# The first step of a fused GELU block by halves of its rows, and its operands in single transposing loads

## Chip, cores and metric

The kernel runs on one core of a Trainium2 chip. The metric is device time in microseconds (us), the median of three runs. The profile is one further execution, taken by the hardware profiler; its span is the time from the first to the last instruction that it records. PE is the matrix engine, DVE the vector engine, ACT the scalar engine, POOL the GpSimd engine, and SP the engine that issues most of the DMA loads.

## What is computed

The reference is the forward pass of a two-layer block with tanh-GELU and all its gradients. The core of it:

```python
h   = einsum("bsd,df->bsf", x, w1) + b1      # B=1, S=2048, D=448, F=1792, all bf16
h   = gelu(h, approximate=True)
out = einsum("bsf,fd->bsd", h, w2) + b2
_out, _vjp = jax.vjp(_f, x, w1, b1, w2, b2)
grads = _vjp(grad_out)                       # for x, w1, b1, w2, b2
```

So there are six matrix products: u = x w1 and out = h w2 forward, the product of grad_out with w2 transposed, the gradient of x from the gated result, and the gradients of w1 and w2 as sums over all rows. The gradients of b1 and b2 are sums over rows.

## The kernel before

**Tiling.** The 2048 rows are four blocks of 512 (SB). F is 14 tiles of 128; a step handles two of them, so a block has 7 steps (NPAIR) and the main loop 28 (g). D is 448, which is three tiles of 128 and a rest of 64 (DL). x, grad_out (g), w1 and w2 transposed (w2T) stand in SBUF with D on the partitions: tiles 0 to 2 are full, tile 3 (KF) is the rest. For x and w1 the three full tiles are columns 64 to 447 and the rest is columns 0 to 63, in partitions 0 to 63; for g and w2T the full tiles are columns 0 to 383, and the rest is in partitions 64 to 127. The two rests therefore use different halves of the array's rows and run beside each other.

**Loads.** `load_x`, `load_g` and `load_w2T` (lines 137 to 156) each issue two transposing DMAs from SP's queue: one of the three full tiles and one of a single tile of 128 columns that covers the rest. SP's queue is in order and carries, one after the other, x and g of block 0, w2T, w2 and w1 piece by piece (lines 170 to 205), then x and g of block 1 and w1 transposed. The first piece of w1 (columns 0 to 255) comes over ACT's queue behind b1, the second over POOL's queue behind a memset. Loads of blocks 2 and 3 are issued in the main loop, in the third step of the block before (line 412). Each load waits until the block that last used its buffer is done with it.

**b1.** It is loaded as one row into one partition (line 171); 14 matmuls of one row against a one (line 184) turn it into a column per tile, which DVE copies to `b1_col` (line 185). Zero matmuls around these ("warm", lines 180 and 187) keep PE busy until the data arrive.

**A step.** `M1(g)` (line 218) is the three full tiles of u for two tiles of F, `rest` (line 229) the two rests of u for the next step and of q for this one, `M4(g)` (line 242) the full tiles of q, the product of g with w2T. ACT copies u with the bias into V (`act_first`, line 248), squares it into A and takes the GELU into the ring hT. DVE forms Bt from A and V (line 269), ACT its tanh (line 272), DVE the slope factor p from A and hT (line 276) and, by lines 277 to 279, t. The gate (`dve_gate`, line 282) multiplies t with q into ghT. V, A, Bt, u and q have one buffer each; t and p have two. The main loop (from line 373) issues for step g: the rests, M4(g), the gate, then the copies, squares and GELU of step g+1, DVE's and ACT's later parts for g+1, the pieces of the output products (`run_pieces`, line 337), and M1(g+2). Every engine works its own queue in the order of issue.

**The first step.** Lines 367 to 372 run ahead of the loop: M1(0) and its rest into two PSUM tiles; `first_step` (line 256), which copies one half of u by ACT and the other by DVE and squares each by itself; tanh, slope and product at full width; then M1(1). In step 0 four keep-warm matmuls (line 384) stand between the rests and M4(0).

**After the loop.** POOL loads x and g again with rows on partitions (lines 422 and 423), SP turns hT back from DRAM (line 435), and PE forms the gradients of w1 (lines 471 and 479) and w2 (line 490). POOL also issues the stores of hT during the loop (`store_h`, line 284) and of the outputs (`evict`, line 321).

Of the kernel before, what the change touches and what calls it, by code (L numbers as in the profile page):

```python
# [8 lines left out]
ACT = mybir.ActivationFunctionType  # L9
# [9 lines left out]
def kernel(  # L19
# [79 lines left out]
    def xq(b):  # L99
        o = (b % 2) * 2 * KD * SB  # L100
        return xg_flat[:, o:o + KD * SB].rearrange("p (k s) -> p k s", k=KD)
# [32 lines left out]

    def load_x(b):
        rows = slice(b * SB, (b + 1) * SB)
        nc.sync.dma_start_transpose(out=xq(b)[:, 0:KF, :], in_=x2[rows, DL:D])
        nc.sync.dma_start_transpose(out=xq(b)[:, KF, :], in_=x2[rows, 0:P])  # L140

    def load_g(b):
        rows = slice(b * SB, (b + 1) * SB)
        nc.sync.dma_start_transpose(out=gq(b)[:, KF, :], in_=g2[rows, DOV:D])
        nc.sync.dma_start_transpose(out=gq(b)[:, 0:KF, :], in_=g2[rows, 0:DM])

    def load_w1(eng, f0, f1):
        eng.dma_start(out=w1_sb[:, 0:KF, f0:f1], in_=w1[DL:D, f0:f1].rearrange("(k p) f -> p k f", p=P))
        eng.dma_start(out=w1_sb[0:DL, KF, f0:f1], in_=w1[0:DL, f0:f1])

    def load_w2(eng, t0, t1):
        eng.dma_start(out=w2_sb[:, t0:t1, :], in_=w2[t0 * P:t1 * P, :].rearrange("(t p) d -> p t d", p=P))

    def load_w2T(f0, f1):
        nc.sync.dma_start_transpose(out=w2T_sb[:, KF, f0:f1], in_=w2[f0:f1, DOV:D])
        nc.sync.dma_start_transpose(out=w2T_sb[:, 0:KF, f0:f1], in_=w2[f0:f1, 0:DM])

    def load_w1T(t0, t1):
        nc.sync.dma_start_transpose(out=w1T_sb[:, t0:t1, :], in_=w1[:, t0 * P:t1 * P])

    warm = T_flat[:, 0:SB]
    ones = T_flat[0:1, SB:SB + 1]
    b1_row = T_flat[0:1, 4 * SB:4 * SB + F]
    nc.vector.memset(warm, 0.0)
    nc.vector.memset(ones, 1.0)
    nc.vector.memset(w128[:], 1.0 / P)

    nc.gpsimd.memset(gh_nat[:, NB - 1, 0:6, :], 0.0)
    load_w1(nc.gpsimd, 256, 512)
    load_x(0)  # L170
    nc.scalar.dma_start(out=b1_row, in_=b1.rearrange("(o f) -> o f", o=1))
    load_w1(nc.scalar, 0, 256)
    nc.scalar.activation(out=T_flat[0:1, SB + 2:SB + 3], in_=ones, func=ACT.Gelu_apprx_tanh)
    load_g(0)
    load_w2T(0, 256)
    load_w2(nc.sync, 0, 2)
    load_w1(nc.sync, 512, 768)
    pw = psum_a.tile([P, SB], F32, name="acc")
    for i in range(7):
        nc.tensor.matmul(pw[:], lhsT=warm[:, 0:P], rhs=warm, start=True, stop=True)  # L180

    pb = psum_a.tile([P, SB], F32, name="acc")
    for ft in range(NF):
        nc.tensor.matmul(pb[:, ft:ft + 1], lhsT=b1_row[:, ft * P:(ft + 1) * P], rhs=ones, start=True, stop=True)
    nc.vector.tensor_copy(out=b1_col[:], in_=pb[:, 0:NF])
    for i in range(3):
        nc.tensor.matmul(pw[:], lhsT=warm[:, 0:P], rhs=warm, start=True, stop=True)
    load_w2T(256, 512)
    load_w2(nc.sync, 2, 4)
    load_w1(nc.sync, 768, 1280)  # L190
    load_w2T(512, 768)
    load_w2(nc.sync, 4, 8)
    load_w2T(768, 1024)
    load_w1(nc.sync, 1280, F)
    load_w2T(1024, 1280)
    load_w2(nc.sync, 8, NF)
    load_w2T(1280, 1536)
    load_x(1)
    load_w2T(1536, F)
# [18 lines left out]
    def M1(g):  # L218
        if g == 0:
            u_of[g] = [psum_a.tile([P, SB], F32, name="acc")[:] for h in range(2)]  # L220
        else:
            u = psum_u.tile([P, 2, SB], F32, name="u")
            u_of[g] = [u[:, h, :] for h in range(2)]
        for h in range(2):
            for kt in range(KF):
                nc.tensor.matmul(u_of[g][h], lhsT=w1_sb[:, kt, cols(g, h)], rhs=xq(g // NPAIR)[:, kt, :],  # L226
                                 start=(kt == 0), stop=False, skip_group_check=True)

    def rest(gu, gg):

        if gg is not None:
            q = psum_g.tile([P, 2, SB], F32, name="q")
            g_of[gg] = q
        for h in range(2):
            if gu is not None:
                nc.tensor.matmul(u_of[gu][h], lhsT=w1_sb[0:DL, KF, cols(gu, h)], rhs=xq(gu // NPAIR)[0:DL, KF, :],  # L236
                                 start=False, stop=True, tile_position=(0, 0), skip_group_check=True)
            if gg is not None:
                nc.tensor.matmul(q[:, h, :], lhsT=w2T_sb[DL:P, KF, cols(gg, h)], rhs=gq(gg // NPAIR)[DL:P, KF, :],
                                 start=True, stop=False, tile_position=(DL, 0), skip_group_check=True)  # L240

    def M4(g):
        for h in range(2):
            for kt in range(KF):
                nc.tensor.matmul(g_of[g][:, h, :], lhsT=w2T_sb[:, kt, cols(g, h)], rhs=gq(g // NPAIR)[:, kt, :],  # L245
                                 start=False, stop=(kt == KF - 1), skip_group_check=True)

    def act_first(g):
        u = u_of.pop(g)
# [3 lines left out]
        nc.scalar.activation(out=A_of(g), in_=V_of(g), func=ACT.Square, scale=math.sqrt(3.0 * GELU_C * GELU_A))  # L253
        nc.scalar.activation(out=hT(g), in_=V_of(g), func=ACT.Gelu_apprx_tanh)  # L254

    def first_step(g):

        u = u_of.pop(g)
        nc.scalar.activation(out=V_of(g)[:, 0, :], in_=u[0], func=ACT.Identity, bias=b1_col[:, 0:1])
        nc.vector.tensor_scalar(out=V_of(g)[:, 1, :], in0=u[1], scalar1=b1_col[:, 1:2], scalar2=None, op0=ALU.add)  # L260
        for h in range(2):
            nc.scalar.activation(out=A_of(g)[:, h, :], in_=V_of(g)[:, h, :], func=ACT.Square,
                                 scale=math.sqrt(3.0 * GELU_C * GELU_A))
            nc.vector.scalar_tensor_tensor(out=B_of(g)[:, h, :], in0=A_of(g)[:, h, :], scalar=3.0 * GELU_C,
                                           in1=V_of(g)[:, h, :], op0=ALU.add, op1=ALU.mult)
        nc.scalar.activation(out=hT(g), in_=V_of(g), func=ACT.Gelu_apprx_tanh)  # L266

    def dve_first(g):
        nc.vector.scalar_tensor_tensor(out=B_of(g), in0=A_of(g), scalar=3.0 * GELU_C, in1=V_of(g), op0=ALU.add, op1=ALU.mult)  # L269
# [9 lines left out]
        nc.vector.tensor_tensor(out=t_of(g), in0=t_of(g), in1=p_of(g), op=ALU.mult)  # L279

    def dve_gate(g):
        nc.vector.scalar_tensor_tensor(out=ghT(g), in0=t_of(g), scalar=1.0, in1=g_of.pop(g)[:], op0=ALU.add, op1=ALU.mult)  # L282

    def store_h(g):
        b, c = blk(g)
# [35 lines left out]
    def evict(un):  # L321
        key = (un.kind, un.b, un.j // 2)
        if key not in stage:
            stage[key] = iop.tile([P, 2, D], BF16, name="io_" + un.kind)
        st = stage[key]
        if un.by_act:
            nc.scalar.copy(out=st[:, un.j % 2, :], in_=un.ps[:, 0:D])
        else:
            nc.vector.tensor_tensor(out=st[:, un.j % 2, :], in0=un.ps[:, 0:D], in1=b2_bc[:], op=ALU.add)  # L329
        dst = out2 if un.kind == "o" else gx2  # L330
        if un.j % 2:
            r0 = un.b * SB + (un.j - 1) * P
            nc.gpsimd.dma_start(out=dst[r0:r0 + 2 * P, :].rearrange("(j p) d -> p j d", p=P), in_=st[:])  # L333

    full = []
# [28 lines left out]
            turns.setdefault(at, []).append((b, c0, c1))  # L364
    stored = 0

    M1(0)
    rest(0, None)
    first_step(0)
    act_second(0)  # L370
    dve_second(0)
    M1(1)
    for g in range(NSTEP):
        b, c = blk(g)
        pieces = [U[k] for k in seq[b] for _ in range(NF)]
        n = len(pieces)
        own = pieces[n * c // NPAIR:n * (c + 1) // NPAIR]
        grown = [U[k] for k in grow[b] for _ in range(2)]
        nxt = g + 1 if g + 1 < NSTEP else None
        rest(nxt, g)  # L380
        if g == 0:

            for i in range(4):
                nc.tensor.matmul(pw[:], lhsT=w1_sb[:, 0, 0:P], rhs=xq(0)[:, 0, :], start=True, stop=True)
        M4(g)
        flush(False)
        dve_gate(g)
        if nxt is not None:
            act_first(nxt)
        flush(True)  # L390
        if nxt is not None:
            dve_first(nxt)
        last = b == 0 and c == NPAIR - 1
        if last:
            run_pieces(grown + own)
            flush(True)
        if nxt is not None:
            act_second(nxt)
            dve_second(nxt)
        if g == NPAIR:  # L400
            run_pieces(grown)
            M1(g + 2)
            run_pieces(own)
        elif not last:
            run_pieces(grown + own)
        if g != NPAIR and g + 2 < NSTEP:
            M1(g + 2)
        for _ in range(2):
            if g >= NPAIR - 1 and stored < g:
                store_h(stored)  # L410
                stored += 1
        if c == 2 and 0 < b < NB - 1:
            load_x(b + 1)
            load_g(b + 1)
        for t in turns.get(g, []):
            turn_gh(*t)
# [2 lines left out]
    flush()  # L419


    nc.gpsimd.dma_start(out=x_all, in_=x2.rearrange("(st p) d -> p st d", p=P))
    nc.gpsimd.dma_start(out=g_all, in_=g2.rearrange("(st p) d -> p st d", p=P))
    for k in "og":
        for j in range(SPB):
            un = U[k, NB - 1, j]
# [103 lines left out]
```

## Time and profile before

| What | Value |
|---|---|
| Median of three runs | 275.95 us (275.45 to 275.96) |
| Profiled execution | 275.59 us |
| Its span | 273.8 us, so 1.79 us lie around it |
| Busy share of the span: PE, DVE, ACT, POOL | 98%, 69%, 52%, 20% |
| Chain that ended last, by engine | PE 82%, DVE 12%, ACT 2%, DMA 2%, issue 1% |
| Transposing loads by SP: x, g, w2T | 8, 8 and 14 issues |
| Data moved | 43.78 MB at a mean of 160 GB/s |

A line of a timeline gives the start and length in us, the engine, the line of the kernel, the operation, what it writes and reads, its shape and how many are merged; in brackets stands how long the engine had been idle before it, and what released it. "SPq" is SP's queue, and the length is then the time that the issue took, not that of the transfer. The chain of waits gives start, length, engine, tile and line of the work that ended last, followed back from the end. Where an engine is busy on this chain, shortening its work there moves the end, until another engine takes its place.

### The profile page before, as it was taken

How to read it: one execution, taken by the hardware profiler on the slowest of the kernel's cores; microseconds unless marked ns; L12 is line 12 of the kernel's file. 1: busy time of each engine (PE TensorE's matmuls, PEld its weight loads, DVE VectorE, ACT ScalarE, POOL GpSimd, SP SyncE). 2: the span in 40 equal slices, each digit the busy share in tenths (PEclk: the TensorE clock that was granted, in tenths of full speed). 3: DMA queues.
4: the chain of work that ended last, by engine and by line, in shares of the span. 5: the costliest groups of instructions: out<-in, count | busy, mean ns of one | idle time of the engine just before them, and what ended most of it. 6: DMA issues, size and time to landing. Idle time of an engine off the chain costs nothing.

```text
span 273.8 us, 3596 instructions
## 1 busy us (share of the span) xinstructions
PE 267.6 (98%) x1406; PEld 123.7 (45%) x1406; DVE 189.3 (69%) x218; ACT 143.7 (52%) x188; POOL 54.6 (20%) x57
## 2 busy tenths in 40 slices
PE   7899999999999999999999999999999999999995
PEld 3343434443444344444444445554445655555552
DVE  0799999999999999999888871139999970000000
ACT  2878879788888778887777740011111221112111
POOL 6000002730301403033031135111700019400000
PEclk9999999999999999999999999999999999999999
DMA  7878979999999928055534339999999931101111
GB/s 164 172 190 193 213 117 170 274 317 246 199 242 203 249 58 163 24 154 122 138 113 79 110 105 217 325 335 241 165 201 273 225 100 57 44 9 50 50 51 35
DMA packets 101379, 43.78 MB, mean 160 GB/s; under 512 B 90353, under 2 KB 97905, under 8 KB 101362
## 3 DMA queue, kind: packets, MB, share of 16 engines
q1 hardware_dynamic: 94272, 26.68, 51.6%
q0 software_dynamic: 4544, 14.92, 16.9%
q10 hardware_dynamic: 2546, 1.95, 2.5%
q8 instruction: 11, 0.18, 0.3%
q14 instruction: 6, 0.05, 0.1%
HBM read 7.00 MB, written 14.23 MB: 78 GB/s over the span
## 4 chain that ended last, share of the span: by engine, by line
PE 82%; DVE 12%; ACT 2%; DMA 2%; issue 1%; DVEq 0%
PE acc L313 27%; PE acc L490 16%; PE acc L471 13%; PE q L245 10%; PE u L226 9%; PE u L236 4%; DVE Bt L269 3%; DVE T L276 3%; DVE ghT_h L282 3%; PE acc L479 2%; DMA xg_h<-in_x_dram 2%; DVE T L279 2%; DVE T L277 1%; DVE T L278 1%; ACT VA L252 1%
## 5 line engine op out<-in xcount | busy, mean ns | idle before, releaser
L313 PE MATMUL acc<-w_gw,hT_h 128*128 128x448 bf16 x224 | 46.3, 352 | 0.2 <-ACT VA L252 0.2
L313 PE MATMUL acc<-w1T_gw,ghT_h 128*128 128x448 bf16 x224 | 45.1, 352 | 0.0
L245 PE MATMUL q<-xg_h,w2T_g 128*128 128x512 bf16 x168 | 41.1, 381 | 0.0
L252 ACT ACTIVATE VA<-u,b_col 128x512 f32<-128x512 f32 x54 | 34.0, 679 | 13.5 <-PE u L236 12.9
L226 PE MATMUL u<-xg_h,w_x 128*128 128x512 bf16 x162 | 39.4, 379 | 0.8 <-DMA w_x<-in_w_dram 0.4
L282 DVE SCALAR_TENSOR_TENSOR ghT_h<-T,q 128x1024 bf16<-128x1024 bf16 x28 | 34.2, 1221 | 8.4 <-PE q L245 7.0
L272 ACT ACTIVATE T<-Bt 128x1024 bf16<-128x1024 f32 x28 | 29.6, 1056 | 13.9 <-DVE Bt L269 13.8
L471 PE MATMUL acc<-gh_nat,w_x 128*128 128x512 bf16 (+1 forms) x192 | 36.7, 353 | 0.0
L276 DVE SCALAR_TENSOR_TENSOR T<-VA,hT_h 128x1024 bf16<-128x1024 f32 x28 | 34.1, 1219 | 0.2 <-ACT hT_h L266 0.2
L269 DVE SCALAR_TENSOR_TENSOR Bt<-VA 128x1024 f32<-128x1024 f32 x27 | 32.9, 1219 | 0.0
L313 PEld LDWEIGHTS <-hT_h 128*128 128x128 bf16 x224 | 21.9, 98 | 22.0 <-issue 0.5
L313 PEld LDWEIGHTS <-ghT_h 128*128 128x128 bf16 x224 | 21.9, 98 | 20.9
L456 DVE TENSOR_TENSOR VA<-VA,gh_nat 128x1792 f32<-128x1792 f32 x14 | 30.0, 2142 | 0.5
L253 ACT ACTIVATE VA<-VA 128x1024 f32<-128x1024 f32 x27 | 28.5, 1057 | 0.9
L254 ACT ACTIVATE hT_h<-VA 128x1024 bf16<-128x1024 f32 x27 | 28.1, 1040 | 0.0
L471 PEld LDWEIGHTS <-w_x 128*128 128x128 bf16 x192 | 18.7, 98 | 17.8 <-issue 0.4
L245 PEld LDWEIGHTS <-w2T_g 128*128 128x128 bf16 x168 | 14.2, 97 | 24.9 <-issue 11.4
L226 PEld LDWEIGHTS <-w_x 128*128 128x128 bf16 x168 | 16.3, 98 | 20.0 <-DMA w_x<-in_w_dram 1.4
L492 ACT CAST w_gw<-acc 128x448 bf16<-128x448 f32 x13 | 6.9, 532 | 32.6 <-PE acc L490 32.6
L333 POOL DMA_DIRECT2D out_dram<-io_o x8 | 5.8, 727 | 90.3 <-DVE io_o L329 48.6
L473 ACT CAST w1T_gw<-acc 128x512 bf16<-128x512 f32 (+1 forms) x12 | 6.3, 532 | 30.1 <-PE acc L471 24.2
L286 POOL DMA_DIRECT2D hT_dram<-hT_h x28 | 20.3, 728 | 1.9 <-DMA out_dram<-io_o 1.9
(60 smaller groups left out, 234.6 us busy)
## 6 DMA issues: line engine op xcount, KB each, us to landing
hT_dram<-hT_h POOLq DMA_DIRECT2D x28, 256.0 KB, 4.5
out_dram<-io_o POOLq DMA_DIRECT2D x8, 224.0 KB, 5.0
out_dram<-io_g POOLq DMA_DIRECT2D x8, 224.0 KB, 3.6
w_x<-in_x_dram POOLq DMA_DIRECT2D x1, 1792.0 KB, 10.8
w2T_g<-in_grad_out_dram POOLq DMA_DIRECT2D x1, 1792.0 KB, 14.7
out_dram<-w_gw SPq DMA_DIRECT2D x4, 336.0 KB, 2.4
w_x<-in_w_dram SPq DMA_DIRECT2D x2, 384.0 KB, 4.0
out_dram<-w1T_gw ACTq DMA_DIRECT2D x2, 384.0 KB, 5.4
```

What stands on the lines that cost most here:

```text
L226: nc.tensor.matmul(u_of[g][h], lhsT=w1_sb[:, kt, cols(g, h)], rhs=xq(g // NPAIR)[:, kt, :], start=(kt == 0), stop=False, skip_group_check= ...
L245: nc.tensor.matmul(g_of[g][:, h, :], lhsT=w2T_sb[:, kt, cols(g, h)], rhs=gq(g // NPAIR)[:, kt, :], start=False, stop=(kt == KF - 1), skip_ ...
L252: nc.scalar.activation(out=V_of(g)[:, h, :], in_=u[h], func=ACT.Identity, bias=b1_col[:, ft:ft + 1])
L253: nc.scalar.activation(out=A_of(g), in_=V_of(g), func=ACT.Square, scale=math.sqrt(3.0 * GELU_C * GELU_A))
L269: nc.vector.scalar_tensor_tensor(out=B_of(g), in0=A_of(g), scalar=3.0 * GELU_C, in1=V_of(g), op0=ALU.add, op1=ALU.mult)
L272: nc.scalar.activation(out=t_of(g), in_=B_of(g), func=ACT.Tanh, scale=-1.0 / 3.0)
L276: nc.vector.scalar_tensor_tensor(out=p_of(g), in0=A_of(g), scalar=GELU_C, in1=hT(g), op0=ALU.add, op1=ALU.mult)
L282: nc.vector.scalar_tensor_tensor(out=ghT(g), in0=t_of(g), scalar=1.0, in1=g_of.pop(g)[:], op0=ALU.add, op1=ALU.mult)
L313: nc.tensor.matmul(self.ps[:, 0:D], lhsT=lhsT, rhs=rhs, start=(ft == 0), stop=(ft == NF - 1 and not bias))
L456: nc.vector.tensor_tensor(out=gsb_v, in0=gsb_v, in1=gh_rows(st, 0, NF), op=ALU.add)
L471: nc.tensor.matmul(psv, lhsT=x_all[:, st, kt * P:(kt + 1) * P], rhs=gh_rows(st, a0, a1), start=(st == 0), stop=(st == NS - 1))
L490: nc.tensor.matmul(ps[:, 0:D], lhsT=h_blk[ft][:, st, :], rhs=g_all[:, st, :], start=(st == 0), stop=(st == NS - 1))
```

## The change

**Loads of four tiles.** x, g and w2T come in one transposing DMA of 512 columns for each row instead of two of 384 and 128. A row has only 448 columns, so the access pattern runs past its end: for g and w2T each row takes the first 64 columns of the next row as well, for x each row begins with the last 64 columns of the row before. Those extra columns fall into partitions that nothing reads. With it the rest of x and w1 moves to tile 0, partitions 64 to 127, and the rest of g and w2T to partitions 0 to 63 of tile 3; `M1` and `rest` follow.

**Fallback and rotation.** Where there is no row before (x of rows 0 to 511) or behind (g of the last rows, the last piece of w2T), two DMAs are issued as until now, and POOL copies the rest into the other half of the partitions. The blocks are rotated: block b of the loop takes rows from (b+1) modulo 4 times 512 on, so that the fallbacks fall on x of block 3 and g of block 2. The second loads of x and g after the loop follow this order in two DMAs each instead of one.

**First step by halves.** x of block 0 comes in two loads of 256 rows; the products, ACT's and DVE's operations, M4(0) and the first gate work on halves of 256 columns, in an order written out by hand.

**b1.** It is loaded as 14 rows of 128 behind the first piece of w1 on ACT's queue; four 32 by 32 transposes of DVE and a copy make the column. The 14 matmuls are gone.

**Warm matmuls.** Seven stand ahead of the products, one between their halves, three ahead of M1(1) and one behind it; the four ahead of M4(0) are gone.

```diff
+    def turn_in(out, src, off):
+        nc.sync.dma_start_transpose(out=out, in_=bass.AP(src.tensor, src.offset + off, [src.ap[0], [1, KD * P]]))
+    def load_x(b, r0=0, r1=SB):
+        src = x2[row0(b) + r0:row0(b) + r1, :]
+        dst = xq(b)[:, :, r0:r1]
+        if row0(b) > 0:
+            turn_in(dst, src, DL - P)
+        else:
+            nc.sync.dma_start_transpose(out=dst[:, 0, :], in_=src[:, 0:P])
+            nc.sync.dma_start_transpose(out=dst[:, 1:KD, :], in_=src[:, DL:D])
+            nc.gpsimd.tensor_copy(out=dst[DL:P, 0, :], in_=dst[0:DL, 0, :])
+    def end_in(dst, src, wrap):
+        if wrap:
+            turn_in(dst, src, 0)
+        else:
+            nc.sync.dma_start_transpose(out=dst[:, KF, :], in_=src[:, DOV:D])
+            nc.sync.dma_start_transpose(out=dst[:, 0:KF, :], in_=src[:, 0:DM])
+            nc.gpsimd.tensor_copy(out=dst[0:DL, KF, :], in_=dst[DL:P, KF, :])
...
-    load_x(0)
-    nc.scalar.dma_start(out=b1_row, in_=b1.rearrange("(o f) -> o f", o=1))
+    load_x(0, 0, HB)
+    load_x(0, HB, SB)
     load_w1(nc.scalar, 0, 256)
+    nc.scalar.dma_start(out=b1_rows[0:NF, :], in_=b1.rearrange("(t p) -> t p", p=P))
...
+        for r0, r1 in ((0, HB), (HB, SB)):          # first_products
+            for h in range(2):
+                for kt in range(KF):
+                    nc.tensor.matmul(u_of[0][h][:, r0:r1], lhsT=w1_sb[:, 1 + kt, cols(0, h)],
+                                     rhs=xq(0)[:, 1 + kt, r0:r1], start=(kt == 0), stop=False, skip_group_check=True)
+            for h in range(2):
+                nc.tensor.matmul(u_of[0][h][:, r0:r1], lhsT=w1_sb[DL:P, 0, cols(0, h)], rhs=xq(0)[DL:P, 0, r0:r1],
+                                 start=False, stop=True, tile_position=(DL, 0), skip_group_check=True)
+            if r0 == 0:
+                keep_warm(1, warm[:, 0:P], warm)
...
+        copy(0)                                     # first_chain: 0 and 1 are the halves
+        square(0)
+        gelu(0)
+        cubic(0)
+        copy(1)
+        square(1)
+        tanh(0)
+        gelu(1)
+        slope(0)
+        cubic(1)
+        tanh(1)
+        times(0)
+        slope(1)
+        times(1)
...
-    M1(0)
-    rest(0, None)
-    first_step(0)
-    act_second(0)
-    dve_second(0)
+    keep_warm(7, warm[:, 0:P], warm)
+    for i in range(P // 32):
+        nc.vector.transpose(out=b1_turned[32 * i:32 * (i + 1), :], in_=b1_rows[:, 32 * i:32 * (i + 1)])
+    nc.vector.tensor_copy(out=b1_col[:], in_=b1_turned[:, 0:NF])
+    first_products()
+    first_chain()
+    keep_warm(3, w1_sb[:, 1, 0:P], xq(0)[:, 1, :])
     M1(1)
+    keep_warm(1, w1_sb[:, 1, 0:P], xq(0)[:, 1, :])
```

In the chain, `copy` takes one half of u by ACT and the other by DVE, `square`, `gelu` and `tanh` are ACT's, `cubic` (Bt), `slope` (p) and `times` (t) are DVE's. In SP's queue the last piece of w2 moves ahead of the fifth piece of w2T.

## The prediction

> **What bounds the kernel now.** I read the page's busy table and chain first, then the chain of waits in order of time, then the timeline of the first 16 us, engine by engine. PE is busy 98% of the span, so only two places can give time: the start, before PE is fed, and the few gaps after it. The chain in order of time (start, length, what) shows which engine carries each stretch:
>
> ```profile
> 0.73 4.96 DMA xg_h<-in_x_dram
> ...
> 5.73 1.46 PE acc L226 x6
> 7.19 0.33 PE acc L236
> ...
> 14.51 1.22 DVE Bt L269
> 15.73 1.13 DVE T L276
> ...
> 47.73 0.69 ACT VA L252
> 48.42 0.04 issue
> 48.46 1.45 PE u L226 x6
> ```
>
> Three stretches are to be seen. Up to 14.51 the first step runs alone: the x load, its products, ACT and DVE. From 14.51 to 47.7 DVE carries the chain, 5.07 us a step without a gap (Bt starts at 14.51, 19.58, 24.65, 29.72). From 48.46 PE runs without a gap to 270.6. PE also runs almost solidly from 11 us: M4's first matmuls start at 11.87, 16.61, 21.36, 26.51, 31.26, 36.01 and 40.75, 4.75 apart but for one 5.15, so PE has 0.32 us a step over DVE. At 48.1 PE waits 0.36 us for the copies of u by ACT, which stand behind DVE's chain. So **the end moves with DVE's start of the second step, Bt at 14.51**, as long as PE's own start moves along: PE may lag DVE by 0.36 us, plus the 0.40 of the 5.15 step if that stall goes (there PE waits until 23.07; the load of w2 tiles 4 to 7 lands at 23.03 by the landing marks).
>
> What sets 14.51 is in the timelines of DVE and PE (start, length, engine, line; in brackets idle time before and its releaser):
>
> ```profile
> 7.54 0.69 ACT L259 ACTIVATE VA<-acc,b_col 128x512 f32<-128x512 f32 x1 [3.70 <-PE acc L236]
> 7.76 0.75 DVE L260 TENSOR_SCALAR VA<-acc,b_col 128x512 f32<-128x512 f32 x1 [2.81 <-PE acc L236]
> 8.93 1.29 DVE L264 SCALAR_TENSOR_TENSOR Bt<-VA 128x512 f32<-128x512 f32 x2 [0.41 <-ACT VA L262]
> 10.39 1.22 DVE L276 SCALAR_TENSOR_TENSOR T<-VA,hT_h 128x1024 bf16<-128x1024 f32 x1 [0.17 <-ACT hT_h L266]
> 13.37 1.22 DVE L282 SCALAR_TENSOR_TENSOR ghT_h<-T,q 128x1024 bf16<-128x1024 bf16 x1 [0.35 <-PE q L245]
> 10.46 0.39 PE L239 MATMUL q<-xg_h,w2T_g 64*128 64x512 bf16 x1 [0.55 <-DMA w2T_g<-in_w_dram]
> 11.00 1.04 PE L384 MATMUL acc<-xg_h,w_x 128*128 128x512 bf16 x4
> 11.87 1.46 PE L245 MATMUL q<-xg_h,w2T_g 128*128 128x512 bf16 x6
> ```
>
> DVE is nearly full from 7.76 on; its gate waits 0.35 us for M4, which ends at 13.33. M4 had waited for w2T, whose main part lands at 11.23, and then for the four keep-warm matmuls. The second path is SP's queue, which issues every load one after the other:
>
> ```profile
> 0.73 1.37 SPq L139 DMA_TRANSPOSE xg_h<-in_x_dram  x1
> 2.15 1.24 SPq L140 DMA_TRANSPOSE xg_h<-in_x_dram  x1
> 3.44 1.25 SPq L144 DMA_TRANSPOSE xg_h<-in_grad_out_dram  x1
> 4.74 2.10 SPq L145 DMA_TRANSPOSE xg_h<-in_grad_out_dram  x1
> 6.88 1.24 SPq L155 DMA_TRANSPOSE w2T_g<-in_w_dram  x1
> 8.17 1.28 SPq L156 DMA_TRANSPOSE w2T_g<-in_w_dram  x1
> ```
>
> A transposing load costs SP 1.24 us for one tile and 1.37 for three; L145 took 2.10 with over 1,100 packets of 256 B still in flight.
>
> **Part 1, the products come earlier.** Now w1 (ACT's queue, issued at 1.29) lands at 5.47 and x's three tiles (issued at 0.73) at 5.69. PE starts at 5.73 and ACT's copy at 7.54: 1.81 us for eight matmuls of 512 columns. In the change w1 goes ahead of b1, so it is issued at 0.74: 0.55 earlier, landing about 4.9, its tail 5.5 (now 6.05). The first half of x is 256 rows by 512 columns, 1,024 packets instead of 1,536. The trace counts 1,024 packets done at 3.98; w1 now competes half a us sooner, so about 4.3; from last packet to landing it takes 0.65 us: 5.0. Bounds: a load of 256 rows by three tiles lands 3.0 us after its issue at best, x's now takes 4.96, so 3.7 to 5.7. The products: six matmuls of half the width at half of 0.216 us, 0.7; the two of L236, the first to its reader 0.42 now and about 0.3 at half width. So the copy could start at 5.0 + 0.7 + 0.3 = 6.0.
>
> b1 comes by DMA (14 rows), four DVE transposes and a copy, in place of 14 matmuls and a copy. Issued third on ACT's queue at about 1.8; the empty queue took 1.5 us to land it, w1's tail 4.26 us, so 3.3 to 6.05; I take 5.5, as it follows that tail. The trace has no DVE transpose; the memset L165 takes 0.06 and the copy L185 0.17, so five instructions lie between 0.3 and 0.85: b1_col at 6.0, at worst 6.9. With both, **the copy starts at 6.2** (6.0 to 6.9) instead of 7.54.
>
> **Part 2, the chain by halves.** From the rows, half sizes: copies 0.47 (ACT) and 0.48 (DVE); ACT on 512 elements 0.62, starting 0.53 apart; DVE's f32 operation 0.69, 0.61 apart (1.29 for two); bf16 operations 0.28 and 0.42. Laid out in the program's order, with 0.03 us for each crossing between engines, from the copy's start: cubic at 1.27, second copy 1.88, slope 2.3, second cubic 3.1, times 3.7, slope 4.35, times 5.2, gates 5.9 and 6.5, and the next Bt at 7.1. Now it is 14.51 - 7.54 = 6.97. So the halves gain nothing inside DVE: six more instructions eat the waits that go (0.41, 0.17 and 0.35). A split costs 2 x 0.61 - 1.14 = 0.08 us by starts, 0.16 by durations. The Trainium skill (Perfetto Trace Analysis, Optimizing Scalar/DVE Operations) puts about 60 ns on each DVE instruction over SBUF and advises grouping where the engine is saturated, which speaks against the halves; by it the six cost 0.36 us, by the row 0.5.
>
> Bt then starts at 6.2 + 7.1 = 13.3 instead of 14.51: **1.2 us earlier**, if M4's halves are ready for the gates at 12.1 and 12.7.
>
> **Part 3, M4's data.** x, g and w2T need four transposing issues instead of six up to w2T. Moving the same bytes, the queue has gaps now (the half us from 9.0 moved 42 GB/s). But g is one load of 2,048 packets. It can stall as L145 did, or w1T's at 43.95, which took 3.06. Lower bound: 1.5 each without a stall, w2T's data by 9.0; upper: g waits for all of x and w2T for nearly all of g, 12.9. I take g issued until 6.5 and w2T until 8.2 to 9.0, landing at 10.2. Then rest 0.55, M4 by halves 1.3 and 0.1 to the reader: 11.5 and 12.15, ahead of the gates. It hides up to a landing of about 10.6; from there each us costs one, and at 11.8 the gain is gone. w1's second load (8.08 from POOL's queue) is unchanged and holds M1(1) at 8.1 to 9.4, before that landing. The five keep-warm matmuls (1.1 us) stand in these gaps, no longer ahead of M4. SP's later loads come 2 to 4 us sooner, which takes the wait at 23.07.
>
> **Part 4, the rest.** The fallback loads (x of the last block, g of the third, the last piece of w2T) put a copy on POOL. The trace has no such copy; its memset of 3,072 elements took 2.66, so 0.1 to 2.7. Queued behind them are the stores of hT and of outputs: the copy for g holds POOL from about 56 to 67, where it idles from 58.8 to 72.6 now; two stores slip, into a ring of twelve. The loads are issued over 20 us ahead of use. x_all lands at 177 and is needed at 185.4; two more POOL issues of 1.15 fit. Work on PE after 48.46 is the same. I cost all this at nothing.
>
> **Sum.** PE's start moves by 11.87 - 10.75 = 1.1 plus the stall of 0.40 plus the 0.36 of slack, more than DVE's 1.2. So 1.2 comes off. The profiled execution took 275.59 (span 273.8 and 1.79 around it): 274.4. The median of the runs, 275.95, lies 0.36 above it: **274.75**.
>
> **Rivals.** (a) M4's data come as late as now, 11.2: M4's second half at 13.35, Bt at 13.95, gain 0.55, down to none at 11.8: 275.4 to 275.95. For it: L145's stall; against: the gaps in the queue. (b) Slower: the same queue at its worst. If each four-tile load waits for nearly all before it, w2T lands at 12.9, M4's second half at 15.0, Bt at 15.6, 1.1 lost: 277.05. It decides from 11.8. For it: L156 at 19.98 stalled 0.8 until 28 packets were left; against: the load of 1,792 packets at 36.19 took 1.47 with 567 ahead. (c) The change does not bring what it says: b1 arrives at 6.05 and holds the copy to 6.9: gain 0.5, 275.45. (d) PE slow at the first products. Matmuls start 0.427 us apart until 3.71 and 0.216 from 4.67; the change leaves PE idle from 4.3 to 5.0. Eight half matmuls at the slow pace cost 0.85, gain 0.35: 275.6. The gap of 0.55 before 10.46 did not slow those after it (379 to 390 ns). The Trainium skill (TensorE: Matmul & The Clock Gate, Part 1) says that the clock falls after an idle window of about 3.4 us and that the window runs free of the kernel's start; by the first the gap is harmless, by the second a slow start stays possible.
>
> **Chances.** Forecast 0.56, (a) 0.19, (b) 0.13, (c) 0.07, (d) 0.05. A measurement here can tell 0.2%, 0.55 us, from no change. Faster: the forecast and a little of (a), (c), 0.6; same 0.25; slower: (b) and what I have not seen, 0.15. The range runs from a gain of 1.75 (copy at 5.8, M4 on time) to a loss of 0.2, with half the spread of the three runs (0.25) on either side: 273.95 to 276.4.
>
> **What would show it.** Right: ACT's first copy near 6.2, Bt of the second step near 13.3, no PE wait near 23, PE solid from about 47.2. Wrong: the first copy waiting on DVE's b1_col; the gate waiting on M4, and M4 on w2T after 11; SP's g load over 3 us; a PE gap after 50.

## The result, and the profile after

| | Before | After |
|---|---|---|
| Median of six runs | 275.85 us (275.45 to 276.19) | 278.10 us (277.07 to 278.27) |
| Ratio | | 1.0076, interval 1.0058 to 1.0093 |
| Profiled execution, its span | 275.59, 273.8 | 278.27, 276.5 |
| First copy by ACT | 7.54 | 9.44 |
| First gate | 13.37 | 15.68 |
| Bt of the second step | 14.51 | 16.87 |

The change makes the kernel 0.76% slower. The forecast was 274.75, with a range up to 276.4: sign and range were both missed. Two of the six runs of e2_warm below (280.83 and 280.91) were in a slower state, so its median is that of the other four.

The chain of waits of the changed kernel in order of time (start, length, engine, what, line) reads like that of before, only later:

```profile
0.73 4.50 DMA xg_h<-in_x_dram
...
5.27 1.44 PE acc L280 x6
6.71 0.54 PE acc L283 x2
7.25 0.54 PE acc L264
7.79 1.28 PE acc L280 x6
9.07 0.55 PE acc L283 x2
...
9.65 0.50 DVE VA L295
...
16.95 1.14 DVE Bt L337
...
50.24 0.69 ACT VA L270
...
50.97 1.24 PE u L239 x5
```

(The last piece ends with the view's window.) x lands at 5.23, early, as meant. But then **both** halves' products stand on the chain before the first copy, at twice their length: 1.44 us for six matmuls of 256 columns, where 0.81 is had at full pace (e3's first half, below). From Bt on nothing is new: M1(9), the PE piece in the last line, starts 34.10 us behind Bt, before 33.95.

The timeline of the first 17 us shows the same from the readers' side (in brackets: idle before, and the releaser):

```profile
5.57 0.85 DVE L442 STREAM_TRANSPOSE T<-T 32x32 bf16<-32x32 bf16 x4 [4.21 <-DMA T<-in_b_dram]
6.45 0.17 DVE L443 CAST b_col<-T 128x14 f32<-128x14 bf16 x1
9.44 0.47 ACT L294 ACTIVATE VA<-acc,b_col 128x256 f32<-128x256 f32 x1 [5.28 <-PE acc L283]
9.65 0.48 DVE L295 TENSOR_SCALAR VA<-acc,b_col 128x256 f32<-128x256 f32 x1 [3.02 <-PE acc L283]
10.89 0.69 DVE L309 SCALAR_TENSOR_TENSOR Bt<-VA 128x512 f32<-128x512 f32 x1 [0.76 <-ACT VA L299]
15.68 1.28 DVE L352 SCALAR_TENSOR_TENSOR ghT_h<-T,q 128x512 bf16<-128x512 bf16 x2
16.87 1.22 DVE L337 SCALAR_TENSOR_TENSOR Bt<-VA 128x1024 f32<-128x1024 f32 x1
```

b1's column is ready at 6.6, so it isn't what ACT waits for. The copy of the *first* half reads 256 columns that were finished at about 7.25; it starts at 9.44, after the second half's last matmuls (9.01 and 9.19). The gate has no bracket: it waits for nothing, so M4, which ends at 15.0, is not late for it. PE's and SP's own timelines show the two other faults:

```profile
5.27 1.44 PE L280 MATMUL acc<-xg_h,w_x 128*128 128x256 bf16 x6 [0.93 <-DMA xg_h<-in_x_dram]
6.65 0.60 PE L283 MATMUL acc<-xg_h,w_x 64*128 64x256 bf16 x2
7.58 1.49 PE L280 MATMUL acc<-xg_h,w_x 128*128 128x256 bf16 x6
9.01 0.61 PE L283 MATMUL acc<-xg_h,w_x 64*128 64x256 bf16 x2
11.36 1.47 PE L239 MATMUL u<-xg_h,w_x 128*128 128x512 bf16 x6 [1.00 <-DMA w_x<-in_w_dram]
3.45 2.82 SPq L145 DMA_TRANSPOSE xg_h<-in_grad_out_dram  x1
6.31 3.60 SPq L145 DMA_TRANSPOSE w2T_g<-in_w_dram  x1
```

PE idles 0.93 us ahead of the first products and runs slow until 9.49, where the trace's record of the full clock begins (before: 4.14). And M1(1), which ran at 8.13 before, waits for w1's second piece until 11.36. The list of DMA issues of the first 14 us (size, us from issue to landing) shows that piece, first in the kernel before, then in the changed one:

```profile
w_x<-in_w_dram POOLq DMA_DIRECT2D x1, 192.0 KB, 4.8
```

```profile
w_x<-in_w_dram POOLq DMA_DIRECT2D x1, 192.0 KB, 8.0
```

So there are three suspects: **A**, the copies wait for the whole PSUM tile and not for their half; **B**, PE is slow at the first products; **C**, the four-tile loads and POOL's load of w1 slow each other. Rivals to these were that the loads alone, b1 alone, or the halves' own extra instructions carry the loss.

### The profile page after: what moved, and what is told of

It is laid out like the page before. It is cut to its first block, busy times and chain, and to the rows that moved or that the text cites. A ratio compares the mean times of both kernels' runs of the same rounds, so it can differ in the third digit from the quotient of the medians.

```text
span 276.5 us, 3604 instructions
## 1 busy us (share of the span) xinstructions
PE 269.4 (97%) x1404; PEld 125.1 (45%) x1404; DVE 191.2 (69%) x229; ACT 144.2 (52%) x191; POOL 57.3 (21%) x62
## 4 chain that ended last, share of the span: by engine, by line
PE 82%; DVE 14%; DMA 2%; ACT 1%; issue 0%; DVEq 0%; ACTq 0%
PE acc L384 27%; PE acc L564 15%; PE acc L545 13%; PE q L258 10%; PE u L239 9%; PE u L248 4%; DVE ghT_h L352 3%; DVE Bt L337 3%; DVE T L344 3%; PE acc L553 2%; DMA xg_h<-in_x_dram 2%; DVE T L347 2%; DVE T L345 1%; PE acc L280 1%; DVE T L346 1%; DVE Bt L309 0%
## 5 line engine op out<-in xcount | busy, mean ns | idle before, releaser
L258 PE MATMUL q<-xg_h,w2T_g 128*128 128x512 bf16 (+1 forms) x174 | 41.1, 373 | 0.0
L352 DVE SCALAR_TENSOR_TENSOR ghT_h<-T,q 128x1024 bf16<-128x1024 bf16 (+1 forms) x29 | 34.2, 1184 | 7.6 <-PE q L258 6.2
L340 ACT ACTIVATE T<-Bt 128x1024 bf16<-128x1024 f32 x27 | 28.5, 1057 | 13.9 <-DVE Bt L337 13.8
L344 DVE SCALAR_TENSOR_TENSOR T<-VA,hT_h 128x1024 bf16<-128x1024 f32 x27 | 32.9, 1218 | 0.0
L398 ACT CAST io_g<-acc 128x448 bf16<-128x448 f32 x16 | 8.3, 520 | 22.6 <-PE acc L384 22.6
```

Source lines behind the costliest of these rows:

```text
L258: nc.tensor.matmul(g_of[g][:, h, r0:r1], lhsT=w2T_sb[:, kt, cols(g, h)], rhs=gq(g // NPAIR)[:, kt, r0:r1], start=False, stop=(kt == KF - 1 ...
L340: nc.scalar.activation(out=t_of(g), in_=B_of(g), func=ACT.Tanh, scale=-1.0 / 3.0)
L344: nc.vector.scalar_tensor_tensor(out=p_of(g), in0=A_of(g), scalar=GELU_C, in1=hT(g), op0=ALU.add, op1=ALU.mult)
L352: nc.vector.scalar_tensor_tensor(out=ghT(g)[:, :, r0:r1], in0=t_of(g)[:, :, r0:r1], scalar=1.0, in1=q[:, :, r0:r1], op0=ALU.add, op1=ALU.mult)
```

## The experiments

Each was run in five rounds beside the kernel before; the ratio is to the runs of before in the same rounds, whose medians were 275.65 to 275.85. "Bt" is the start of Bt of the second step in the profiled execution; the profiled time of all fourteen kernels is Bt plus 261.1 to 261.6, so Bt tells the mechanism and the ratio the size.

| Kernel | First copy | Bt | Median | Ratio to before |
|---|---|---|---|---|
| before | 7.54 | 14.51 | 275.85 | |
| after | 9.44 | 16.87 | 278.10 | 1.0076 (1.0058 to 1.0093) |
| b6_loads | 9.70 | 16.41 | 276.32 | 1.0033 (1.0013 to 1.0054) |
| b7_b1 | 8.21 | 15.18 | 276.68 | 1.0029 (1.0015 to 1.0043) |
| h2_halves | 8.54 | 15.86 | 276.66 | 1.0031 (1.0019 to 1.0044) |
| e1_banks | 7.24 | 15.79 | 277.09 | 1.0059 (1.0041 to 1.0077) |
| e2_warm | 8.14 | 15.86 | 277.07 | 1.0053 (1.0033 to 1.0073) |
| e3_w1_act | 9.28 | 16.71 | 277.93 | 1.0084 (1.0064 to 1.0104) |
| e4_all | 7.52 | 15.46 | 276.63 | 1.0035 (1.0022 to 1.0047) |
| g0_quarters | 7.17 | 17.15 | 278.75 | 1.0115 (1.0091 to 1.0139) |
| g1_split | 6.97 | 14.31 | 276.25 | 1.0012 (1.0002 to 1.0022) |
| h3_warm_act | 8.82 | 16.15 | 277.25 | 1.0059 (1.0047 to 1.0072) |
| h5_quarters_act | 7.73 | 14.96 | 275.86 | 1.0005 (0.9996 to 1.0014) |
| g3_b1pool_w1act | 6.93 | 14.26 | 275.81 | 1.0003 (0.9994 to 1.0011) |

### Each suspect undone in the changed kernel

**e1_banks** gives each half of the rows a PSUM tile of its own, with both column tiles in it. This kernel and e4_all leave out a part of the sums of step 0, probably in the first column tile, because the second starts its sum in the same tile while the first is open (no run isolates this); the instructions are the same.

```diff
-        u_of[0] = [psum_a.tile([P, SB], F32, name="acc")[:] for h in range(2)]
         for r0, r1 in ((0, HB), (HB, SB)):
+            u = psum_a.tile([P, SB], F32, name="acc").rearrange("p (h r) -> p h r", h=2)
+            u_of[r0] = u
```

> The changed kernel, but each half of the first products has a PSUM tile of its own (both column tiles of F of one half side by side), where the change put both halves of one column tile into one. Theory 1 (three delays stand one behind the other at the start: ACT's first copy waits for the last matmul of the second half because both halves share a tile; PE runs at its slow pace until 9.5 us; and the data of the second step come late, w1's second piece at 11.3): the first copy starts at 7.0 instead of 9.44, but M4 still ends at 15.0, so the gate cannot start before 15.05, and Bt of the second step at 16.25 instead of 16.87: 0.6 faster than the changed kernel, 277.5. Theory 2 (the loads of four tiles alone set the start): the first copy moves, the time does not, 278.1. Theory 3 (the halves cost, because DVE has more instructions): same as theory 2 or less than 0.3 gained.

Measured 277.09. The first copy goes from 9.44 to 7.24, straight behind the first half's matmuls. But half of the gain is lost again: ACT and DVE now read one tile, and DVE waits for ACT, twice. The timeline:

```profile
7.24 0.47 ACT L295 ACTIVATE VA<-acc,b_col 128x256 f32<-128x256 f32 x1 [3.10 <-PE acc L284]
7.75 0.48 DVE L296 TENSOR_SCALAR VA<-acc,b_col 128x256 f32<-128x256 f32 x1 [1.16 <-ACT VA L295]
10.11 0.48 DVE L296 TENSOR_SCALAR VA<-acc,b_col 128x256 f32<-128x256 f32 x1 [0.49 <-ACT VA L295]
```

From copy to Bt it takes 8.55 us in place of 7.43; the slow products of the second half (ACT's second copy, at 9.60, waits 0.18 us for them) and M4 (the gate waits 0.22 us) have a part in this. A is real, and its cure needs a tile for each reader as well.

**e2_warm** runs ten warm matmuls ahead of the products instead of seven, which fills the idle 0.93 us.

```diff
-    keep_warm(7, warm[:, 0:P], warm)
+    keep_warm(10, warm[:, 0:P], warm)
```

> The changed kernel with ten instead of seven warm matmuls ahead of the first products, so that PE is not idle between 4.35 and 5.27. Theory 1: PE comes to its full pace one decision earlier, before 7.5 us; the products of the second half end at 7.5 to 8.2 instead of 9.2 and the first copy starts there; M4's end at 15.0 binds next: Bt at 16.25, 0.6 faster, 277.5. Theory 2 and 3: 278.1, no change.

Measured 277.07, more of a gain than was expected. The full clock is recorded from 6.12, the second half's products take 0.82 us instead of 1.49, and the copy starts at 8.14. B is real: 1.3 us at the copy. Of this 1.0 arrives at Bt, because M4 now is late (the gate waits 0.30 us for it): M4 needs q's rest first, and that waits for w2T until 12.60. So C shows as soon as B goes, here in the four-tile load of w2T.

```profile
5.42 1.17 PE L280 MATMUL acc<-xg_h,w_x 128*128 128x256 bf16 x6
7.07 0.82 PE L280 MATMUL acc<-xg_h,w_x 128*128 128x256 bf16 x6
10.00 1.47 PE L239 MATMUL u<-xg_h,w_x 128*128 128x512 bf16 x6 [1.04 <-DMA w_x<-in_w_dram]
12.60 0.39 PE L250 MATMUL q<-xg_h,w2T_g 64*128 64x512 bf16 x1 [0.46 <-DMA w2T_g<-in_w_dram]
```

**e3_w1_act** moves w1's second piece from POOL's queue to ACT's, behind the first piece and b1.

```diff
-    load_w1(nc.gpsimd, 256, 512)
...
+    load_w1(nc.scalar, 256, 512)
```

> The changed kernel with the second piece of w1 (columns 256 to 511) issued on ACT's queue behind the table load instead of on POOL's. Theory 1: the piece lands by 9 instead of 11.3 and M1(1) moves up, but the first copy still starts at 9.4 and the time stays at 278.1, within 0.2. Theory 2: the start follows these data, 1 to 2 us faster, 276.5 to 277. Theory 3: 278.1.

Measured 277.93, no gain to be told from after. The transfers are quicker (the table of packets below), but PE falls into another hole: it waits 1.18 us for x's first half and 0.71 for the second, and the clock, granted at 4.54, is taken away again for one stretch. The windows view (window, length, busy time of each engine, granted clock, DMA share, GB/s) cut at the marks of the clock:

```profile
core 0: us, PE busy (x) PEld busy (x) DVE busy (x) ACT busy (x) POOL busy (x), PEclk, DMA share, GB/s
4.54:7.95 3.41, 1.72 (x12) 0.94 (x12) 0.98 (x5) 0.00 (x0) 0.00 (x0) 1.00 1.20 216
7.95:11.36 3.41, 3.41 (x13) 1.23 (x11) 1.11 (x3) 1.76 (x4) 0.00 (x0) 0.50 1.04 221
11.36:14.77 3.41, 3.41 (x24) 1.89 (x23) 3.31 (x9) 3.08 (x7) 0.00 (x0) 1.00 1.00 212
```

So e3 did not test C by its time; it shows B a second time.

**e4_all** has the three edits together.

> The three edits together. Theory 1: the first copy at 6.2 to 6.5, M4 ended by 13.2 to 13.5, Bt of the second step at 14.5 to 14.7, so about as the kernel before: 275.9 to 276.2. Theory 2: as the run with w1 on ACT's queue alone, 276.5 to 277. Theory 3 (six more DVE instructions): 276.5 or more, DVE full from the first copy on with a chain over 7.5 us.

Measured 276.63, where 275.9 to 276.2 was expected. The copy now waits for b1 (b1_col is written from 7.24 to 7.41), and DVE still waits for ACT at the shared tile: 7.94 us from copy to Bt.

### The parts of the change alone, in the kernel before

**b6_loads** takes only the four-tile loads, the rotation and the fallbacks (the first x as one load of 512 rows).

> The kernel before with nothing but the loads changed: x, g and w2T in single transposing loads of four tiles (x of block 0 whole), blocks rotated, POOL's copies. First step, b1 and warm matmuls as before. Theory 1 (in its form after the first four runs: the whole difference stands in the start of Bt of the second step, and the time is that start plus 261.1 to 261.4 us): g's load of 2,048 packets holds SP's queue and shares the DMA engines with w1's second piece from POOL's queue, which lands at 10 to 11.5 instead of 8.1; M1(1) and behind it M4 come later, M4 ends at 14.5 to 15, Bt at 15.7 to 16.3: 277 to 277.5, so these loads alone make the kernel 1 to 2 us slower. Rival 2 (the loads are neutral, all of the loss is in the halves and the slow PE): 275.4 to 276, as the kernel before.

Measured 276.32, between the two theories. Its twelve runs scatter from 275.94 to 278.84, and the profiled one, at 277.72, is among the slower: in it PE is slow until 10.56, and its six first products of 512 columns take 2.72 us instead of 1.46. So its Bt of 16.41, near the expected 16.3, comes from another cause than the expected one, and stands for the slower of its runs only. w1 suffers less here: its large packets run from 7.43 to 9.37, not from 5.75 to 10.92, perhaps because g's issue is held (3.99 us, until 6.19), and M1(1) starts at 10.02.

**b7_b1** takes only b1: 14 rows behind w1, four transposes by DVE.

```diff
+    nc.scalar.dma_start(out=b1_rows[0:NF, :], in_=b1.rearrange("(t p) -> t p", p=P))
...
-    for ft in range(NF):
-        nc.tensor.matmul(pb[:, ft:ft + 1], lhsT=b1_row[:, ft * P:(ft + 1) * P], rhs=ones, start=True, stop=True)
-    nc.vector.tensor_copy(out=b1_col[:], in_=pb[:, 0:NF])
+    for i in range(P // 32):
+        nc.vector.transpose(out=b1_turned[32 * i:32 * (i + 1), :], in_=b1_rows[:, 32 * i:32 * (i + 1)])
+    nc.vector.tensor_copy(out=b1_col[:], in_=b1_turned[:, 0:NF])
```

> The kernel before with nothing but b1 changed: 14 rows behind w1's first piece on ACT's queue, four DVE transposes and a copy, no b1 matmuls; 7 and 3 warm matmuls now back to back. Theory 1: b1_col at 6.4, w1 earlier by half a us, but x lands at 5.7 as before and the products end at 7.5: no change, 275.5 to 276. Rival 2 (b1 by this way is late and holds ACT's copy): first copy after 8, 0.5 to 1 slower.

Measured 276.68; no change was expected, a miss, and the rival's first copy after 8 came true. b1 lands at 7.0 and not before 6, so the column is ready only at 8.1. But x's rest is late too, and by the bracket the copy waits for its matmul; the two end within 0.1 us of each other, so this run does not tell which of them costs the time:

```profile
7.94 0.18 DVE L186 CAST b_col<-T 128x14 f32<-128x14 bf16 x1
8.21 0.69 ACT L260 ACTIVATE VA<-acc,b_col 128x512 f32<-128x512 f32 x1 [4.07 <-PE acc L237]
7.78 0.59 PE L237 MATMUL acc<-xg_h,w_x 64*128 64x512 bf16 x2 [0.97 <-DMA xg_h<-in_x_dram]
```

**h2_halves** takes only the halves (products, chain, M4, gate), with the shared tiles; loads and b1 as before.

> The kernel before with nothing but the first step changed: products, ACT's and DVE's operations, M4(0) and the first gate by halves of the rows in the change's order, both halves of a column tile in one PSUM tile. Loads, b1 and warm matmuls as before. Theory 1: the first copy waits for the second half (7.5 to 7.8, about as before), and DVE's chain from there to Bt of the second step is 7.3 to 7.5 us, as in the changed kernel, instead of 6.97: Bt at 15.0, 0.5 slower, 276.3. Rival (the halves cost nothing where PE runs at its pace): 275.8.

Measured 276.66 (the profiled run 277.32). The chain from copy to Bt takes 7.32 us, as expected, 0.35 more than before. But the first copy starts at 8.54 (behind both halves) and not at 7.5 to 7.8, since here too PE is slow at first: the clock is recorded from 6.78, three warm matmuls take 1.46 us instead of 0.82, and the products start at 6.00.

```profile
4.74 1.46 PE L187 MATMUL acc<-T 128*128 128x512 bf16 x3
6.00 1.21 PE L269 MATMUL acc<-xg_h,w_x 128*128 128x256 bf16 x6
```

So there is neither C nor a late b1 here, but some of B, and the run does not separate it from the halves. As measured, **each of the three parts loses about 0.3% alone** (0.33, 0.29 and 0.31%); together they lose 0.76%.

### Pairs that isolate A and C

**g0_quarters** has four PSUM tiles, one for each half and column tile, the warm matmuls in a q tile to make room, and ten of them (the diff of the tiles stands at h5 below); **g1_split** is g0 with g and w2T in two loads of one and three tiles again.

```diff
-            turn_in(dst, src, 0)
+            nc.sync.dma_start_transpose(out=dst[:, KF, :], in_=bass.AP(src.tensor, src.offset + DM, [src.ap[0], [1, P]]))
+            nc.sync.dma_start_transpose(out=dst[:, 0:KF, :], in_=src[:, 0:DM])
```

> The changed kernel with a PSUM tile for each of the four quarters of the first products (two halves of rows, two tiles of F), so that neither a copy waits for the other half nor DVE's copy for ACT's, and with ten warm matmuls. The bank for the warm matmuls is borrowed from q. Theory 1: the first copies of ACT and DVE start at 6.5 to 7.0 side by side, DVE could have its gate by 13.2, but M4 still ends near 14.5 because w1's second piece lands after 10: Bt at 15.5 to 15.9, 276.7 to 277.2. Rival 2 (loads neutral): Bt at 14.0 to 14.3, 275.3.

> As the run with quarters, but g and w2T again in two loads of one and three tiles each (the single tile still past the rows' ends, so that the layout stays). Theory 1: the issue of g's load shortens to 1.25 and 1.3 to 2.1, w1's second piece lands by 8.5 to 9, M4 ends by 13.4, Bt at 14.3 to 14.7: 275.5 to 276. Rival 2: no difference to the run with quarters.

g0 measured 278.75, a larger loss than expected and slower than the change itself although its copy starts at 7.17: with A and most of B gone, C decides. M1(1) waits for w1; q's rest, which M4 needs, starts at 13.89, as w2T lands (issued at 6.05, landed 7.8 us later); and the gate waits 2.57 us for M4. Here g0's timeline, then g1's:

```profile
12.03 1.47 PE L239 MATMUL u<-xg_h,w_x 128*128 128x512 bf16 x6 [2.74 <-DMA w_x<-in_w_dram]
13.89 0.39 PE L250 MATMUL q<-xg_h,w2T_g 64*128 64x512 bf16 x1
15.94 1.29 DVE L353 SCALAR_TENSOR_TENSOR ghT_h<-T,q 128x512 bf16<-128x512 bf16 x2 [2.57 <-PE q L258]
3.45 2.55 SPq L145 DMA_TRANSPOSE xg_h<-in_grad_out_dram  x1
6.05 4.73 SPq L145 DMA_TRANSPOSE w2T_g<-in_w_dram  x1
```

```profile
9.00 1.46 PE L240 MATMUL u<-xg_h,w_x 128*128 128x512 bf16 x6
13.11 1.28 DVE L354 SCALAR_TENSOR_TENSOR ghT_h<-T,q 128x512 bf16<-128x512 bf16 x2
4.76 1.78 SPq L160 DMA_TRANSPOSE xg_h<-in_grad_out_dram  x1
7.87 1.44 SPq L160 DMA_TRANSPOSE w2T_g<-in_w_dram  x1
```

One edit, 2.84 us at Bt and 2.50 in the medians (278.75 to 276.25). Part of the 2.50 may be the clock: four of g0's six runs were granted only 0.994 over their span, and the other two took 277.94 and 278.53, 1.7 and 2.3 us more than g1. h5, below, is a second such pair with g0: only w1's second piece moves from POOL's queue to ACT's, and the loads keep their four tiles. Bt comes at 14.96, the median is 275.86, and w2T lands 3.5 us after its issue at 7.72. So the loss needs both, the four-tile loads and POOL's load beside them. That is C. What moved is in the trace's packet records, here as KB ended in each us, SP's queue / the queue with w1's second piece (POOL's; ACT's in e3):

```
        before     after     e3 (ACT)    g0       g1
5-6     232/0      164/0     111/97     175/4    140/16
6-7      31/224     44/84    105/126     28/70    59/126
7-8     123/0       69/64    235/0       70/64    62/42
8-9     274/0       65/42    211/0       69/30   111/40
9-10     87/0      129/10    213/0       66/26   279/0
```

Before, SP's queue stood in the stalled issue of L145 (4.74 to 6.84) while POOL's load ran: it moved 224 KB in one us, its 64 large packets at 209 ns each. In the change the transposing load runs beside it: both together move 107 to 139 KB per us, the 64 packets take 411 ns each (500 in g0, 368 in g1) and end at 10.92 instead of 6.91. On ACT's queue the same bytes beside a transposing load move at 208 to 231 KB per us in e3 and 169 to 198 in h5.

**h3_warm_act** is the change with the edits of e2 and e3; **h5_quarters_act** is h3 with the four tiles of g0.

```diff
-        u_of[0] = [psum_a.tile([P, SB], F32, name="acc")[:] for h in range(2)]
         for r0, r1 in ((0, HB), (HB, SB)):
+            u = [psum_a.tile([P, SB], F32, name="acc")[:, 0:HB] for h in range(2)]
+            u_of[r0] = u
...
-    pw = psum_a.tile([P, SB], F32, name="acc")
+    pw = psum_g.tile([P, 2, SB], F32, name="q")[:, 0, :]
```

> The changed kernel with ten warm matmuls and with w1's second piece on ACT's queue; the halves still share PSUM tiles. Theory 1: x's second half lands at 7.6 because w1's second piece comes beside it, the products end at 8.6 and the first copies start at 8.7, after the second half: Bt at 16.0 to 16.2, 277.2 to 277.5. Rival (the shared tile costs nothing once PE is fast): copies at 7.2 to 7.5, 276.2.

> As the run before it with a PSUM tile for each quarter of the first products: only the sharing of the tiles is different. Theory 1: the first copies wait for b1_col alone, 7.4 to 7.5, ACT and DVE side by side; chain 7.3: Bt at 14.8, 276.0 to 276.2. Rival: no difference between the two.

277.25 against 275.86: 1.39 us for A alone, since only the tiles differ (with them the place of the warm matmuls' result). h3's timeline, then h5's:

```profile
8.82 0.47 ACT L294 ACTIVATE VA<-acc,b_col 128x256 f32<-128x256 f32 x1 [4.67 <-PE acc L283]
6.83 0.39 PE L283 MATMUL acc<-xg_h,w_x 64*128 64x256 bf16 x2
8.50 0.39 PE L283 MATMUL acc<-xg_h,w_x 64*128 64x256 bf16 x2
```

```profile
7.73 0.47 ACT L295 ACTIVATE VA<-acc,b_col 128x256 f32<-128x256 f32 x1 [3.58 <-DVE b_col L444]
7.46 0.17 DVE L444 CAST b_col<-T 128x14 f32<-128x14 bf16 x1
6.79 0.39 PE L284 MATMUL acc<-xg_h,w_x 64*128 64x256 bf16 x2
```

In both, the first half's last two matmuls start near 6.8. In h3 the copy starts 0.32 us after the first of the *second* half's last two (8.50); in h5 it waits only for b1's column, although there the second half ends later still (its last two start at 8.94).

**g3_b1pool_w1act** is h5 with b1 as the first load of POOL's queue instead of the second of ACT's.

```diff
+    nc.gpsimd.dma_start(out=b1_rows[0:NF, :], in_=b1.rearrange("(t p) -> t p", p=P))
...
-    nc.scalar.dma_start(out=b1_rows[0:NF, :], in_=b1.rearrange("(t p) -> t p", p=P))
```

> As the run with quarters and w1's second piece on ACT's queue, with b1 issued first on POOL's queue, ahead of the memset. Theory 1: b1 lands by 4.5, the first copies start with the products of the first half, 6.6 to 7.0, DVE has its gate ready by 12.9, M4 ends at 13.0 (g and w2T land by 11): Bt at 14.2 to 14.3, about as the kernel before: 275.4 to 275.8. Rival (loads of four tiles still late, M4 after 14): 276.5.

Measured 275.81, ratio 1.0003: all faults mended, and still only equal to before. The copy starts at 6.93, 0.61 ahead of before; its chain to Bt takes 7.33 instead of 6.97, so 0.36 is given back by the halves; of the 0.25 us left at Bt (14.26 for 14.51), 0.22 goes between Bt and the end (261.30 for 261.08).

## Why the prediction was wrong

**The bound was right.** "The end moves with DVE's start of the second step" holds in fourteen kernels within 0.55 us, while Bt itself ranges from 14.26 to 17.15. What failed is the time of that start: 16.87 for 13.3.

**The step that failed is "the copy starts at 6.2".** It started at 9.44. The sum was x at 5.0, products 0.7, the last to its reader 0.3, and 0.2 for b1. Found: the first product at 5.27 (0.27 more), the first half's products until 7.25 (1.98 for 1.0: fault B), and then 2.19 us more until the second half was done (fault A), less the 0.2 for b1, which wasn't needed: 3.24 in all. At full pace the 1.0 is good: in g3 products start at 5.87 and the copy at 6.93, 1.06 later. The missing term was a dependency that no row of before could show, because there the reader wants the whole tile anyway; but the diff showed it: `u_of[0]` is one tile for both halves. None of the four rivals has it. The Trainium skill (PSUM — Partial Sum Buffer, PSUM bank collisions raise a hardware error) says that engines must be kept apart by bank and quadrant, whatever columns they touch, two readers included. The trace agrees on both counts as far as waits go: 2.19 us of waiting for matmuls into columns that the copy does not read, and 0.5 us of DVE behind ACT in e1. This rule spoke against the change and was not weighed.

**Rival (d), PE slow, happened** and was given a chance of 0.05 and a price of 0.85 us. Its price was for half of the products; with A both halves lie ahead of the copy, and e2 gains 1.30 there. The idle time was forecast as well (4.3 to 5.0; found 4.35 to 5.27), but given little weight. Stepping back 3.41 us from each mark of the clock shows how near it was: PE was busy 87% of the window ahead of the mark in before (0.72 to 4.14) and 93% in e3, and both were granted; in the change 73% (2.67 to 6.08) was not, and the next window had to pass. The busy share alone does not decide, though: in b6 a window of 94% (3.73 to 7.14, with b1's 14 small matmuls in it) was not granted either. And where the windows lie differs from execution to execution: before, b7, h2 and b6 all start the same warm matmuls at 1.18, and the clock is recorded from 4.14, 4.87, 6.78 and 10.56. So how much B costs is in part luck; after and e2 can be compared because their windows happen to lie alike (2.67 to 6.08, 2.71 to 6.12). Whoever removes 14 matmuls and brings x 0.5 us forward moves just this share. The Trainium skill (TensorE: Matmul & The Clock Gate, Part 1) has the window run free of the kernel's start; the trace agrees, with these differing marks, and they are 3.41 us apart in e3.

**Rival (b), the loads' queue, came true nearly to its numbers, and the first fault hid it.** SP's issues took 2.82 for g (forecast until 6.5, found 6.27) and 3.60 for w2T (until 8.2 to 9.0, found 9.91). w2T, issued at 6.31, landed 6.4 us later, at 12.7; the forecast had 10.2 and rival (b) 12.9, with M4's end at 15.0, where it was found. So the landing in part 3 failed as well. (b) also missed a victim: "w1's second load is unchanged", said part 3; it landed at 11.3 instead of 8.1, and M1(1), which the prediction saw at 8.1 to 9.4, started at 11.36 and stood ahead of M4 on PE until 12.8. In the change itself the gate comes behind all this, at 15.68; by g0 and g1 it is worth 2 to 2.5 us where nothing hides it. An early copy alone does not win, then: g0's starts at 7.17, and its Bt at 17.15.

**Rival (c), b1 late, was sized well.** The column was ready at 6.62 (forecast 6.0, at worst 6.9); the five instructions took 1.02 us, over the bound of 0.85: a transpose took 0.20, not 0.06 to 0.17. It binds only where the copy is early (e4, h5), and nearly so where b1 lands at 7.0 (b7).

**The chain by halves was right.** Forecast 7.1 from copy to Bt and no gain inside DVE; found 7.43, and 7.32 to 7.34 in g1, g3, h2 and h3, against 6.97 before. From DVE's first copy to Bt, DVE is busy 6.33 us instead of 5.77 with six more instructions: 0.56, near what the rows gave (0.5). The prediction took 0.36 from the Trainium skill (Perfetto Trace Analysis, Optimizing Scalar/DVE Operations), at about 60 ns each; but that section has about 125 ns for PSUM, and two of the six, a copy and a gate, read PSUM. So the estimate by that page is 0.49, and the measured 0.56 is near it. The waits hardly shrink, 0.98 us to 0.89: the three of before go, but the first Bt now waits 0.76 for ACT's square of the half, which wants both copies.

**POOL's copies cost almost nothing**, as forecast. The first, at 31.98, lengthens one step of DVE from 5.07 to 5.23 us; by the chain, Bt beside it takes 1.29 for 1.14. In POOL's and DVE's timelines:

```profile
31.98 0.40 POOL L163 COPY w2T_g<-w2T_g 64x256 bf16<-64x256 bf16 x1 [27.14 <-DMA w2T_g<-in_w_dram]
32.09 1.37 DVE L337 SCALAR_TENSOR_TENSOR Bt<-VA 128x1024 f32<-128x1024 f32 x1
```

This is half of the 0.32 us by which the change is longer behind Bt. The other 0.17 lies behind the last matmul: from there to the end of the span it is 3.38 us, before 3.20; what made it longer was not traced.

**The range's lower end** has a slip that played no part: by the prediction's own sum a copy at 5.8 gains 1.6 us, not 1.75.

## What to carry to other kernels

Splitting an operation shortens a start only if its reader can be released by the part: look first whether the parts have tiles of their own, one for each pair of writer and reader, else the first reader waits for the last writer and the split only adds instructions. Before bringing a load forward or making it larger, list what every other queue moves in those microseconds, for a stall that looks like waste may be what keeps a neighbour's transfer fast. And a start is a balance of PE's early busy share, loads and small operands: mend all of them and count again, since here the repaired version only equals the old one.

## What the runs showed of the hardware beyond expectation

- **Queues are not alike beside a transposing load.** With w1's second piece in POOL's queue, all queues together moved 107 to 139 KB per us from 6 to 10 us in the change and 81 to 134 from 6 to 11 in g0; with the same piece in ACT's queue, 208 and 231 in the two us in which it ran (e3). The Trainium skill (DMA: Bandwidth & Descriptors, Issuing engines are not separate DMA queues) says that starting DMAs from several engines saves only the time to start them; by g0 and h5 the choice of queue moved Bt by 2.19 us, though ACT's load ran earlier (5 to 7 us in e3) and beside x, so that the moment is part of the difference.
- **The issue of a four-tile transposing load** took 1.30 us at the least (12.02 in the change) and up to 4.73, while g's and w1's packets were still moving (g0).
- **The clock can fall without an idle window.** In e3 it was halved after a window in which PE was busy for 1.72 of 3.41 us. The Trainium skill (TensorE: Matmul & The Clock Gate, Part 1) ties the fall to an idle window; here PE's longest idle time in that window was 0.99 us (4.54 to 5.53). In g0 a window of 49% (10.30 to 13.71) did not lower it, so the busy share alone does not settle when it falls. e3's profiled run was granted 0.994 over its span; four runs of g0, two of b6, one of b7 (0.993) and two of e2 (0.994 and 0.988) are as low or lower, and none of before is below 0.998.
- **A DVE transpose of 32 by 32** took 0.20 us, 0.85 for four in a row.
